# Chunked attention and a soft mixture of experts on one core: the work of a step in another order, and the softmax subtraction written in address order

## The chip, the cores and the metric

The kernel runs on one core of a Trainium2 chip. A core has a matrix engine (TensorE, shown as PE, its weight loads as PEld), a vector engine (VectorE, DVE), a scalar engine (ScalarE, ACT), GpSimd (POOL), and SyncE (SP), whose queue here issues every data transfer. Each engine takes its own instructions strictly in the order in which they are written, and waits on semaphores for what others produce. Matrix products land in PSUM, everything else lies in SBUF. The metric is the device time of one execution in microseconds; less is better.

## What is computed

Attention over 4 batches, 8 heads, 768 positions of 64 values, in chunks of 32 queries. Each chunk sees 8 memory keys, 16 positions to its left, itself, and 8 to its right. The result, as a matrix `x` of 3072 rows and 512 columns, goes through a soft mixture of 8 experts with 4 slots each.

```python
# attention, per chunk
scores = scale * np.matmul(q_c, k_full.transpose(0, 1, 3, 2))
a = np.exp(scores - np.max(scores, axis=-1, keepdims=True))
a = a / (np.sum(a, axis=-1, keepdims=True) + 1e-09)
out[:, :, c_start:c_end] = np.matmul(a, v_full)
...
# experts
logits = x @ phi
d = np.exp(logits - logits.max(0, keepdims=True))
d /= d.sum(0, keepdims=True) + 1e-09
slot_input = d.T @ x
...
h = np.maximum(slot_input[e] @ w1[e], 0.0)
slot_out[e] = h @ w2[e]
...
return (c @ slot_out).astype(np.float32)
```

Here `c` is the softmax of the logits over the slots. All numbers are float32.

## The kernel before

The attention is cut into 12 units of 256 rows (`NU`), numbered 0 to 11, and each step `i` of the main loop (lines 387 to 423) finishes unit `i`. One unit passes through these functions, one TensorE group or one short run of VectorE and ScalarE work each:

- `scores` (line 237, TensorE): 32 matrix products into the one PSUM tile `s`. Every product is float32 and stands as two in the trace, so a unit shows 64.
- `softmax` (line 250, VectorE): `mx`, the maxima of 64 keys each, then two subtractions `p` of 128x512 elements, one for each half of the heads, from PSUM `s` to SBUF `p`. The four blocks of keys of a chunk are stored interleaved, so that a subtraction writes every second word of `p`. Before the change the last loop of the subtraction runs over 32 neighbouring words of PSUM, and writes every fourth word of SBUF; the other block follows in a second sweep.
- `exponent` (line 269, ScalarE): the exponential of `p`, in place.
- `normalizer` (line 272, VectorE): `z`, sums of `p` that read every second word, and their reciprocals.
- `transpose_p` (line 279, TensorE, then ScalarE): `pt_ps` in PSUM, and its copies `pt` in SBUF.
- `values` (line 291, TensorE): 64 products in the trace, into the one PSUM tile `a`; `normalize` (line 308, VectorE): `x`, from `a` and `z`.
- `transpose_x` (line 316, TensorE, then ScalarE): `xt_ps` and its copies `xT`.

Two units make a group `G` of 512 rows. In even steps from 2 on the group's `logits` (line 324, TensorE, `l`) follow with `dispatch_max` (VectorE, `stats` and the copy `lT`) and `dispatch_exp` (ScalarE, `d`); in odd steps `dispatch_t` (line 354, `dt_ps`, `dT`), `dispatch` (`D_ps`) and `dispatch_sum` (`D_sb`, VectorE).

`s` and `a` have one buffer each (two PSUM banks each); the other four banks go round among all smaller PSUM tiles. So `scores` of a unit waits for the subtractions of the unit before, and `values` for the `normalize` before it. The order of the calls in the loop body is the order on every engine, because each call is kept in program order (class `InOrder`).

All transfers go through SyncE's queue, in the order of the calls. A unit loads 512 KB of queries, 560 to 592 KB of keys, 512 KB of values (`vw`, tile `v..0`) and 256 KB of values more (`vx`), which go into the tile `v..1` after GpSimd has copied `v..0` into it (`share_v`). There are three buffers of each (`NB`). With the 64 KB of `phi` these are 22.9 MB in all (MB of a million bytes). Expert weights come in 64 pieces of 512 KB, 32 of `w1` and 32 of `w2`, into slabs: 14 of their own (`NW`), then the buffers of keys, queries, values and `x` as units finish with them, 35 in all. `load_w(upto)` (line 176) issues pieces up to a count: 1.5 a step in the first eight steps, later all for which the table `usable` names a slab. `vx` of a unit stands behind the weights of its step in the queue.

After the loop come the last group, the merge of the groups' maxima, the two layers of the experts (`h`, `so`) and two halves of the output (`o`), each stored by a transfer. There a slab is refilled as soon as its piece has been used.

Of the kernel before, what the change touches and what calls it, by code (L numbers as in the profile page):

```python
# [10 lines left out]
F32 = mybir.dt.float32  # L11
AF = mybir.ActivationFunctionType
# [3 lines left out]
P = 128  # L16
B, H, S, D = 4, 8, 768, 64
NPAIR = H // 2
# [4 lines left out]
NU = B * UPB  # L23
# [20 lines left out]
NEG = -1.0e30  # L44
PIECE = 1024
NB = 3
NW = 14
W0 = 1
WRATE = 1.5
WLAST = 8  # L50
# [19 lines left out]
def tile_attn_softmoe(  # L70
# [68 lines left out]
    def load_v(u):  # L139
        e = v_t[u % NB][0]  # L140
        for h in range(2):
            sp.dma_start(e[h:P:2, h], vw[u, 64 * h:64 * h + 64])
# [12 lines left out]
    for d in range(NB):  # L155
        u = NU - NB + d
        flat = k_t[u % NB].rearrange("p a n -> p (a n)")
        freed += [(u - 2, flat[:, 0:PIECE]), (u - 2, flat[:, PIECE:2 * PIECE])]
        freed += [(u - 2, q_t[u % NB].rearrange("p g n -> p (g n)"))]
        if d:  # L160
            freed += [(u, v_t[u % NB][o][:, a]) for o in range(2) for a in range(2)]
    flat_x = [t.rearrange("p u n -> p (u n)") for t in x_t]
    last = (NG - 1) % 2
    freed += [(NU, flat_x[1 - last][:, 0:PIECE]), (NU, flat_x[1 - last][:, PIECE:2 * PIECE])]
    freed += [(NU + 1, flat_x[last][:, 0:PIECE]), (NU + 1, flat_x[last][:, PIECE:2 * PIECE])]
    usable = {i: NW for i in range(NU + 2)}
    for since, s in sorted(freed, key=lambda f: f[0]):
        slabs.append(s)
        for i in range(since, NU + 2):
            usable[i] = len(slabs)  # L170

    pieces = [("w1", e, kc) for e in range(E) for kc in range(NKC)]
# [64 lines left out]
    def scores(u):  # L237
        s_ps = ps.tile([P, NSUB, NPAIR, 2, 2 * CHUNK], F32, tag="S", name=f"s{u}")
        for s in range(NSUB):
            for g in range(NPAIR):  # L240
                for j in range(4):
                    pe.matmul(
                        s_ps[32 * j:32 * j + 32, s, g],
                        lhsT=q_t[u % NB][:, g, P * s + 32 * j:P * s + 32 * j + 32],
                        rhs=key_columns(u, 4 * s + j, g),
                        start=True, stop=True,
                    )
        return s_ps

    def softmax(u, s_ps):  # L250
        if u % UPB == 0:
            dve.memset(s_ps[0:32, 0, :, :, 0:LEFT], NEG)
        if u % UPB == UPB - 1:
            dve.memset(s_ps[96:128, NSUB - 1, :, :, CHUNK - RIGHT:CHUNK], NEG)
        flat = s_ps.rearrange("p s g h n -> p (s g h) n")
        mx = wk.tile([P, 16, 1], F32, tag="mx", name=f"mx{u}")
        dve.tensor_reduce(out=mx[:, :, 0], in_=flat, axis=AX.X, op=ALU.max)
        p = wk.tile([P, 8, 4 * CHUNK], F32, tag="p", name=f"p{u}")
        for h in range(2):
            dve.tensor_tensor(  # L260
                out=p.rearrange("p m (j s h) -> p h m s j", s=2, h=2)[:, h],
                in0=s_ps.rearrange("p s g h (b j) -> p h (s g) b j", b=2)[:, h],
                in1=mx.rearrange("p (m h) o -> p h m o", h=2)[:, h].rearrange(
                    "p m (o z) -> p m o z", z=1).broadcast_to([P, 8, 2, CHUNK]),
                op=ALU.subtract,
            )
        pexp[u] = p

    def exponent(u):
        act.activation(out=pexp[u], in_=pexp[u], func=AF.Exp, scale=SCALE)  # L270

    def normalizer(u):
        z = wk.tile([P, 16, 1], F32, tag="z", name=f"z{u}", bufs=3)
        dve.tensor_reduce(out=z.rearrange("p (m h) o -> p m (h o)", h=2), in_=pexp[u].rearrange("p m (n h) -> p m h n", h=2), axis=AX.X, op=ALU.add)
        dve.tensor_scalar_add(z, z, 1e-9)
        dve.reciprocal(out=z, in_=z)
        rz[u] = z

    def transpose_p(u):
        pt = []  # L280
        pv = pexp[u]
        for s in range(NSUB):
            t_ps = row(4 * P, f"pt_ps{u}_{s}")
            for g in range(NPAIR):
                pe.transpose(t_ps[:, P * g:P * g + P], pv[:, NPAIR * s + g, :], ident)
            t = wk.tile([P, NPAIR, P], F32, tag=f"pt{s}", name=f"pt{u}_{s}")
            act.copy(out=t.rearrange("p g n -> p (g n)"), in_=t_ps)
            pt.append(t)
        return pt
# [18 lines left out]
    def normalize(u, a_ps):  # L308
        dve.tensor_tensor(
            out=x_of(u).rearrange("p s (m d) -> p (s m) d", d=D),  # L310
            in0=a_ps.rearrange("p s g h d -> p (s g h) d"),
            in1=rz[u].broadcast_to([P, 16, D]),
            op=ALU.mult,
        )

    def transpose_x(u):
        for s in range(NSUB):
            t_ps = row(4 * P, f"xt_ps{u}_{s}")
            for kc in range(NKC):
                pe.transpose(t_ps[:, P * kc:P * kc + P], x_of(u)[:, s, P * kc:P * kc + P], ident)  # L320
            xT[2 * u + s] = wk.tile([P, NKC, P], F32, tag="xT", name=f"xT{u}_{s}", bufs=4)
            act.copy(out=xT[2 * u + s].rearrange("p g n -> p (g n)"), in_=t_ps)

    def logits(G):
        l_ps = row(P, f"l{G}")
        for kc in range(NKC):
            for g in range(4):
                pe.matmul(
                    l_ps[32 * g:32 * g + 32, :],
                    lhsT=phi_sb[:, kc, :],  # L330
                    rhs=xT[4 * G + g][:, kc, :],
                    start=(kc == 0), stop=(kc == NKC - 1),
                )
        return l_ps
# [6 lines left out]
    def dispatch_max(G, l_ps):  # L341
        dve.tensor_reduce(out=nmx[G], in_=l_ps, axis=AX.X, op=ALU.max, negate=True)
        if G:
            dve.tensor_tensor(out=nmx[G], in0=nmx[G], in1=nmx[G - 1], op=ALU.min)
        dve.tensor_copy(out=lT[:, G, :], in_=l_ps)

    def dispatch_exp(G, l_ps):
        d = wk.tile([P, P], F32, tag="d", name=f"d{G}")
        act.activation(out=d, in_=lT[:, G, :], func=AF.Exp, bias=nmx[G], scale=1.0, accum_out=zg[G])
        dexp[G] = d  # L350
        if G:
            act.activation(out=alpha[G], in_=nmx[G - 1], func=AF.Exp, bias=nmx[G], scale=-1.0)
# [7 lines left out]
    def dispatch(G):  # L360
        D_ps = row(DM, f"D_ps{G}")
        for g in range(4):
            pe.matmul(
                D_ps[32 * g:32 * g + 32, :],
                lhsT=dT[G][:, 32 * g:32 * g + 32],
                rhs=x_t[G % 2][:, g, :],
                start=True, stop=True,
            )
        return D_ps
# [5 lines left out]
    def dispatch_sum(G, D_ps):  # L375
        if G == 0:
            dve.tensor_copy(out=D_sb, in_=D_ps)
        else:
            dve.scalar_tensor_tensor(out=D_sb, in0=D_sb, scalar=alpha[G], in1=D_ps, op0=ALU.mult, op1=ALU.add)

    for u in range(2):
        softmax(u, scores(u))
        load_k(u + NB)
        load_q(u + NB)
        exponent(u)
    normalizer(0)
    for i in range(NU):
        G = (i - 2) // 2 if i >= 2 else None
        first = i % 2 == 0
        pt = transpose_p(i)  # L390
        if i >= 1:
            transpose_x(i - 1)
        if G is not None and not first:
            dispatch_t(G)
        if i + 2 < NU:
            softmax(i + 2, scores(i + 2))
            exponent(i + 2)
        a_ps = values(i, pt)
        normalize(i, a_ps)
        if i + 1 < NU:  # L400
            normalizer(i + 1)
        if G is not None and first:
            l_ps = logits(G)
            dispatch_max(G, l_ps)
            dispatch_exp(G, l_ps)
        if G is not None and not first:
            D_ps = dispatch(G)
            dispatch_z(G)
            dispatch_sum(G, D_ps)
        if i + 3 < NU:  # L410
            first_k(i + 3)
        if i + 2 < NU:
            share_v(i + 2)
        if i + 5 < NU:
            load_k(i + 5)
            load_q(i + 5)
        if i + 3 < NU:
            load_v(i + 3)
        load_w(W0 + int(WRATE * (i + 1)) if i < WLAST else usable[i])
        if i + 2 < NU:  # L420
            load_vx(i + 2)
        if i == NU - NB + 1:
            pool.memset(hT, 0.0)
# [1 line left out]
    l_ps = logits(NG - 1)  # L425
    dispatch_max(NG - 1, l_ps)
    dispatch_exp(NG - 1, l_ps)
    load_w(usable[NU])

# [15 lines left out]
    wrow = wk.tile([P, 1], F32, tag="wrow", name="wrow", bufs=1)  # L447
    act.activation(out=wrow, in_=nm, func=AF.Exp, bias=nmt, scale=-1.0)
    dispatch_sum(NG - 1, D_ps)
    load_w(usable[NU + 1])  # L450
    selw = wk.tile([P, NSLOT], F32, tag="selw", name="selw", bufs=1)
    dve.tensor_scalar(out=selw, in0=sel, scalar1=wrow, scalar2=None, op0=ALU.mult)
    si_ps = row(NKC * NSLOT, "si_ps").rearrange("p (c s) -> p c s", c=NKC)
# [184 lines left out]
```

## Time and profile before

| what | value |
|---|---|
| median of 3 runs | 205.89 us (204.71 to 209.38) |
| profiled execution, its own time | 206.37 us |
| its span, first to last instruction | 204.6 us |
| TensorE busy | 153.1 us, 75% |
| VectorE busy | 100.4 us, 49% |
| ScalarE busy | 61.0 us, 30% |
| GpSimd busy | 33.6 us, 16% |
| moved by transfers | 63.11 MB, mean 309 GB/s |

A time in the rows counts from the span's start. In the chain of waits each piece is what the next one waited for; the pieces are merged, and in order of time. In the timeline a row is a run of equal instructions, and the bracket at its end is the idle time just before it with what ended that. A matrix product's end is modelled and reaches into the next product, so that for TensorE the distance between two starts tells more than a duration. All instructions bear line 64, that of the helper which records them, so they are told apart by the names of their tiles.

### The profile page before, as it was taken

Reading aid. Unit: us, or ns where it says so; the run is one execution under the profiler, and the core shown is the slowest. Engines: PE = TensorE matmul, PEld = TensorE weight load, DVE = VectorE, ACT = ScalarE, POOL = GpSimd, SP = SyncE. Lnnn points to the kernel's source line nnn. Section 1 sums busy time; section 2 is a strip of 40 time slices with the busy share of each in tenths; the row PEclk is TensorE's granted clock in tenths of the full one; section 3 lists DMA queues with packets and bytes.
Section 4 is the critical chain, followed back from the end, with each engine's and each line's share of the span. In section 5 each row is a group of like instructions: output and inputs, shape, how many; then the busy total and the mean of one; then the engine's idle time right before and its main releaser. Section 6 shows DMA issues by size and latency. Waiting matters only on the chain.

```text
span 204.6 us, 6085 instructions
## 1 busy us (share of the span) xinstructions
PE 153.1 (75%) x2639; PEld 110.0 (54%) x2639; DVE 100.4 (49%) x168; ACT 61.0 (30%) x115; POOL 33.6 (16%) x42
## 2 busy tenths in 40 slices
PE   5629767887894888579858587688999976699551
PEld 5518656776693757467756374444556642344220
DVE  7063887392879097748926653321460103310331
ACT  7510351425142532335250505300222203210331
POOL 5343134032122402141233000000000000000000
PEclk9999999696999699999988999955999996559955
DMA  6998999998599479925889969996999999998275
GB/s 231 341 350 275 302 390 353 324 308 285 169 325 390 181 211 346 395 105 175 291 242 380 420 192 323 307 385 203 295 407 419 405 405 410 409 412 356 114 301 210
DMA packets 18218, 63.11 MB, mean 309 GB/s; under 512 B 3088, under 2 KB 3088, under 8 KB 18192
## 3 DMA queue, kind: packets, MB, share of 16 engines
q1 hardware_dynamic: 18192, 62.73, 84.2%
q8 instruction: 21, 0.34, 0.7%
q14 instruction: 5, 0.04, 0.1%
HBM read 56.43 MB, written 6.29 MB: 307 GB/s over the span
## 4 chain that ended last, share of the span: by engine, by line
PE 49%; DVE 26%; DMA 15%; ACT 4%; issue 3%; SPq 1%; ACTq 0%; POOLq 0%
PE s L64 12%; PE so L64 8%; PE h L64 8%; DVE p L64 7%; DMA k<-in_k_dram 7%; PE o L64 6%; DVE x L64 5%; DMA v<-in_vx_dram 5%; DVE mx L64 4%; PE a L64 4%; PE xt_ps L64 4%; DMA w<-in_w_dram 4%; DVE z L64 3%; DVE w L64 2%; PE D_ps L64 1%
## 5 line engine op out<-in xcount | busy, mean ns | idle before, releaser
L64 PE MATMUL s<-k,q 128*32 128x128 f32 x768 | 32.6, 340 | 7.4 <-DMA k<-in_k_dram 5.3
L64 PEld LDWEIGHTS s<-k,q 128*32 128x32 f32 x768 | 27.9, 138 | 10.8 <-issue 7.3
L64 POOL COPY v<-v 128x2048 f32<-128x2048 f32 x12 | 22.8, 1898 | 58.5 <-DMA v<-in_vw_dram 26.6
L64 ACT ACTIVATE p<-p 128x1024 f32<-128x1024 f32 x12 | 12.7, 1058 | 63.4 <-DVE p L64 63.4
L64 PE MATMUL a<-v,pt 128*32 128x128 f32 x768 | 24.1, 273 | 3.4 <-DMA v<-in_vx_dram 2.4
L64 PE MATMUL xt_ps<-ident,x 128*128 128x128 f32 x96 | 14.9, 288 | 15.4 <-DVE x L64 7.2
L64 DVE TENSOR_TENSOR p<-s,mx 128x512 f32<-128x512 f32 x24 | 24.6, 1108 | 0.4
L64 PEld LDWEIGHTS a<-v,pt 128*32 128x32 f32 x768 | 21.6, 111 | 4.2 <-issue 3.9
L64 DVE TENSOR_REDUCE mx<-s 128x16 f32<-128x1024 f32 x12 | 14.7, 1225 | 13.4 <-PE s L64 13.1
L64 PEld LDWEIGHTS xt_ps<-ident,x 128*128 128x128 f32 x96 | 10.5, 144 | 19.7 <-DVE x L64 9.7
L64 PE MATMUL o<-shl,v 32*128 32x256 f32 x96 | 12.7, 612 | 8.7 <-DVE w L64 3.9
L64 DVE TENSOR_TENSOR x<-a,z 128x1024 f32<-128x1024 f32 x12 | 14.6, 1217 | 7.3 <-PE a L64 7.3
L64 PE MATMUL pt_ps<-ident,p 128*128 128x128 f32 x96 | 14.1, 292 | 1.0 <-issue 1.0
L64 DVE TENSOR_REDUCE z<-p 128x16 f32<-128x1024 f32 x12 | 14.5, 1208 | 0.0
L64 PEld LDWEIGHTS pt_ps<-ident,p 128*128 128x128 f32 x96 | 11.0, 147 | 6.3 <-PE a L64 2.5
L64 ACT COPY xT<-xt_ps 128x512 f32<-128x512 f32 x24 | 13.0, 601 | 2.8 <-PE xt_ps L64 2.8
L64 PEld LDWEIGHTS o<-shl,v 32*128 32x128 f32 x96 | 5.3, 262 | 15.4 <-DVE w L64 6.5
L64 ACT COPY pt<-pt_ps 128x512 f32<-128x512 f32 x24 | 12.6, 576 | 0.0
L64 DVE MEMSET s<- 32x128 f32 (+1 forms) x8 | 1.1, 138 | 23.3 <-PE s L64 23.3
L64 PE MATMUL l<-xT,phi_sb 128*32 128x128 f32 x192 | 7.5, 274 | 2.4 <-issue 2.3
L64 DVE COPY so_sb<-so 128x256 f32<-128x256 f32 x2 | 0.8, 424 | 15.4 <-PE so L64 15.4
L64 PE MATMUL h<-w,siT 128*32 128x256 f32 x112 | 8.2, 455 | 0.0
(96 smaller groups left out, 157.9 us busy)
## 6 DMA issues: line engine op xcount, KB each, us to landing
w<-in_w_dram SPq DMA_DIRECT2D x28, 512.0 KB, 7.0
v<-in_w_dram SPq DMA_DIRECT2D x14, 512.0 KB, 7.7
q<-in_qT_dram SPq DMA_DIRECT2D x12, 512.0 KB, 6.1
v<-in_vw_dram SPq DMA_DIRECT2D x24, 256.0 KB, 5.5
k<-in_w_dram SPq DMA_DIRECT2D x12, 512.0 KB, 10.2
v<-in_vx_dram SPq DMA_DIRECT2D x24, 128.0 KB, 5.9
q<-in_w_dram SPq DMA_DIRECT2D x6, 512.0 KB, 10.3
out_dram<-w SPq DMA_DIRECT2D x6, 512.0 KB, 2.9
```

Source lines behind the costliest of these rows:

```text
L64: return self.tc.keep_in_program_order(f(*args, **kwargs))
```

## The change

The edits, in four parts:

1. In a step TensorE now runs: transpose of the old `x` (unit `i-1`), `values(i)`, the logits or the dispatch, `scores(i+2)`, and transpose of `p` for unit `i+1`, which was the first group of step `i+1` before. VectorE runs `normalize(i)`, the group's work, `softmax(i+2)` and `normalizer(i+1)`. ScalarE runs `exponent(i+1)` a step later than before.
2. `load_v(i+3)` moves up, to right behind `normalize(i)`, and is followed by a first `load_w`; a second `load_w` stays at the end of the step. The table `usable` counts half steps, and frees the key and query buffers half a step earlier.
3. `dispatch_exp` reads the logits from PSUM, not from the copy `lT`. The copies `pt` have one buffer instead of two, which makes room for a 15th weight slab; there are then 36 slabs.
4. The subtraction's loops are swapped: the two blocks alternate for every key, so that it reads PSUM with jumps of 32 words (128 bytes) and back, and writes every second word of `p` in rising order.

```diff
-NW = 14
+NW = 15
...
-        freed += [(u - 2, flat[:, 0:PIECE]), (u - 2, flat[:, PIECE:2 * PIECE])]
-        freed += [(u - 2, q_t[u % NB].rearrange("p g n -> p (g n)"))]
+        freed += [(2 * u - 3, flat[:, 0:PIECE]), (2 * u - 3, flat[:, PIECE:2 * PIECE])]
+        freed += [(2 * u - 3, q_t[u % NB].rearrange("p g n -> p (g n)"))]
         if d:
-            freed += [(u, v_t[u % NB][o][:, a]) for o in range(2) for a in range(2)]
+            freed += [(2 * u, v_t[u % NB][o][:, a]) for o in range(2) for a in range(2)]
...
-                out=p.rearrange("p m (j s h) -> p h m s j", s=2, h=2)[:, h],
-                in0=s_ps.rearrange("p s g h (b j) -> p h (s g) b j", b=2)[:, h],
+                out=p.rearrange("p m (j s h) -> p h m j s", s=2, h=2)[:, h],
+                in0=s_ps.rearrange("p s g h (b j) -> p h (s g) j b", b=2)[:, h],
...
-            t = wk.tile([P, NPAIR, P], F32, tag=f"pt{s}", name=f"pt{u}_{s}")
+            t = wk.tile([P, NPAIR, P], F32, tag=f"pt{s}", name=f"pt{u}_{s}", bufs=1)
...
-        act.activation(out=d, in_=lT[:, G, :], func=AF.Exp, bias=nmx[G], scale=1.0, accum_out=zg[G])
+        act.activation(out=d, in_=l_ps, func=AF.Exp, bias=nmx[G], scale=1.0, accum_out=zg[G])
...
         softmax(u, scores(u))
         load_k(u + NB)
         load_q(u + NB)
-        exponent(u)
+        if u == 0:
+            exponent(u)
+    pt = transpose_p(0)
     normalizer(0)
     for i in range(NU):
...
-        pt = transpose_p(i)
         if i >= 1:
             transpose_x(i - 1)
+        if i + 1 < NU:
+            exponent(i + 1)
         if G is not None and not first:
             dispatch_t(G)
-        if i + 2 < NU:
-            softmax(i + 2, scores(i + 2))
-            exponent(i + 2)
         a_ps = values(i, pt)
-        normalize(i, a_ps)
-        if i + 1 < NU:
-            normalizer(i + 1)
         if G is not None and first:
             l_ps = logits(G)
+        if G is not None and not first:
+            D_ps = dispatch(G)
+        normalize(i, a_ps)
+        if i + 3 < NU:
+            load_v(i + 3)
+        load_w(W0 + int(WRATE * (i + 0.5)) if i < WLAST else usable[2 * i])
+        if G is not None and first:
             dispatch_max(G, l_ps)
             dispatch_exp(G, l_ps)
         if G is not None and not first:
-            D_ps = dispatch(G)
             dispatch_z(G)
             dispatch_sum(G, D_ps)
+        if i + 2 < NU:
+            softmax(i + 2, scores(i + 2))
+        if i + 1 < NU:
+            pt = transpose_p(i + 1)
+            normalizer(i + 1)
```

TensorE, step 3 (units 2 to 5; the number behind a tile's name is its unit or group, the last number its buffer; `values` of unit 3 goes on in rows that are left out). Before:

```order
L64 MATMUL pt_ps3_0_597<-ident_94,p3_406 128x128 x4
L64 MATMUL pt_ps3_1_604<-ident_94,p3_406 128x128 x4
L64 MATMUL xt_ps2_0_611<-ident_94,x1_77 128x128 x4
L64 MATMUL xt_ps2_1_618<-ident_94,x1_77 128x128 x4
L64 MATMUL dt_ps0_625<-ident_94,d0_584 128x128
L64 MATMUL s5_629<-k2_69,q2_66 32x128 x32
L64 MATMUL a3_669<-v00_70,pt3_0_602 32x128
...
L64 MATMUL D_ps0_707<-x0_76,dT0_627 32x512 x4
```

After, the same step up to the transposes of unit 4's `p`:

```order
L64 MATMUL xt_ps2_0_611<-ident_95,x1_77 128x128 x4
L64 MATMUL xt_ps2_1_618<-ident_95,x1_77 128x128 x4
L64 MATMUL dt_ps0_626<-ident_95,d0_544 128x128
L64 MATMUL a3_630<-v00_70,pt3_0_589 32x128
...
L64 MATMUL D_ps0_663<-x0_76,dT0_628 32x512 x4
L64 MATMUL s5_673<-k2_69,q2_66 32x128 x32
L64 MATMUL pt_ps4_0_712<-ident_95,p4_581 128x128 x4
L64 MATMUL pt_ps4_1_719<-ident_95,p4_581 128x128 x4
```

`scores` of unit 5 went from ahead of `values` of unit 3 to behind it and behind the dispatch, and the transposes of `p` of unit 4 close the step in which those of unit 3 had opened it.

VectorE, the same step. Before:

```order
L64 TENSOR_REDUCE mx5_663<-s5_629 128x16
L64 TENSOR_TENSOR p5_665<-s5_629,mx5_663 128x8x2x32 x2
L64 TENSOR_TENSOR x1_77<-a3_669,z3_561 128x1024
L64 TENSOR_REDUCE z4_703<-p4_523 128x16
L64 TENSOR_SCALAR z4_703<-z4_703 128x16
L64 RECIPROCAL z4_703<-z4_703 128x16
L64 COPY D_sb_93<-D_ps0_707 128x512
```

After:

```order
L64 TENSOR_TENSOR x1_77<-a3_630,z3_598 128x1024
L64 COPY D_sb_94<-D_ps0_663 128x512
L64 MEMSET s5_673 32x8x8
L64 TENSOR_REDUCE mx5_707<-s5_673 128x16
L64 TENSOR_TENSOR p5_709<-s5_673,mx5_707 128x512 x2
L64 TENSOR_REDUCE z4_726<-p4_581 128x16
L64 TENSOR_SCALAR z4_726<-z4_726 128x16
L64 RECIPROCAL z4_726<-z4_726 128x16
```

`x` of unit 3 and the group's sum moved ahead of unit 5's maxima and subtractions; the subtraction's output is now one run of 512.

SyncE's queue, steps 8 and 9: from unit 11's `vw` (tile `v20`) to unit 11's `vx` (tile `v21`). Before:

```order
L64 DMA v20_74<-in_vw_dram 64x1024 x2
L64 DMA w13_91<-in_w1_dram 128x1024
L64 DMA k0_67<-in_w1_dram 128x1024 x2
L64 DMA q0_64<-in_w1_dram 128x1024
L64 DMA k1_68<-in_w1_dram 128x1024 x2
L64 DMA q1_65<-in_w1_dram 128x1024
L64 DMA v11_73<-in_vx_dram 32x1024 x2
L64 DMA k2_69<-in_w1_dram 128x1024 x2
L64 DMA q2_66<-in_w1_dram 128x1024
L64 DMA v21_75<-in_vx_dram 32x1024 x2
```

After:

```order
L64 DMA v20_74<-in_vw_dram 64x1024 x2
L64 DMA w13_91<-in_w1_dram 128x1024
L64 DMA w14_92<-in_w1_dram 128x1024
L64 DMA k0_67<-in_w1_dram 128x1024 x2
L64 DMA q0_64<-in_w1_dram 128x1024
L64 DMA k1_68<-in_w1_dram 128x1024 x2
L64 DMA q1_65<-in_w1_dram 128x1024
L64 DMA v11_73<-in_vx_dram 32x1024 x2
L64 DMA k2_69<-in_w1_dram 128x1024 x2
L64 DMA q2_66<-in_w1_dram 128x1024
L64 DMA v21_75<-in_vx_dram 32x1024 x2
```

Seven pieces of weights stood ahead of unit 10's `vx` (tile `v11`), now eight; the first five of these, and the `vw`, are issued in the middle of step 8, where all stood at its end before.

## Rows read from the trace of the kernel before

**Rows 1.** Page of the profile, part 2: 40 slices of 5.1 us each.

```profile
PEclk9999999696999699999988999955999996559955
...
GB/s 231 341 350 275 302 390 353 324 308 285 169 325 390 181 211 346 395 105 175 291 242 380 420 192 323 307 385 203 295 407 419 405 405 410 409 412 356 114 301 210
```

**Rows 2.** Chain of waits, units 4 and 5: start us, us, what.

```profile
57.62 1.93 PE s L64 x64
...
59.62 0.18 DVE s L64
...
61.08 2.16 DVE p L64 x2
63.24 1.05 DVE x L64
...
66.25 0.21 DVE lT L64
...
67.69 0.33 PE dt_ps L64
68.02 3.57 PE s L64 x64
...
77.26 1.93 PE s L64 x64
```

**Rows 3.** Timeline, TensorE: start us, us, engine, line, operation, out<-in, shapes, count.

```profile
73.10 1.03 PE L64 MATMUL D_ps<-x,dT 128*32 128x512 f32 x8
...
93.29 1.09 PE L64 MATMUL pt_ps<-ident,p 128*128 128x128 f32 x8
...
94.22 1.16 PE L64 MATMUL xt_ps<-ident,x 128*128 128x128 f32 x8
...
95.31 1.95 PE L64 MATMUL s<-k,q 128*32 128x128 f32 x64
...
97.08 1.93 PE L64 MATMUL a<-v,pt 128*32 128x128 f32 x64
...
98.83 1.06 PE L64 MATMUL l<-xT,phi_sb 128*32 128x128 f32 x32
```

**Rows 4.** Groups of VectorE by form: busy us, mean ns | idle before, releaser.

```profile
L64 DVE TENSOR_TENSOR p<-s,mx 128x512 f32<-128x512 f32 x24 | 24.6, 1108 | 0.4
L64 DVE TENSOR_REDUCE mx<-s 128x16 f32<-128x1024 f32 x12 | 14.7, 1225 | 13.4 <-PE s L64 13.1
...
L64 DVE TENSOR_REDUCE z<-p 128x16 f32<-128x1024 f32 x12 | 14.5, 1208 | 0.0
...
L64 DVE TENSOR_REDUCE stats<-l 128x1 f32<-128x128 f32 x6 | 1.4, 239 | 2.2 <-PE l L64 2.2
...
L64 DVE TENSOR_TENSOR v<-c_ps,cm 128x384 f32<-128x384 f32 x2 | 1.1, 558 | 0.1
...
L64 DVE TENSOR_REDUCE nms<-nm_ps 32x32 f32<-32x128 f32 x1 | 0.3, 279 | 1.0 <-PE nm_ps L64 1.0
```

**Rows 5.** Timeline around units 9 to 11 and the experts, SyncE's queue and TensorE.

```profile
99.06 1.12 SPq L64 DMA_DIRECT2D v<-in_vw_dram  x2
...
106.44 1.46 SPq L64 DMA_DIRECT2D v<-in_vx_dram  x2
...
117.65 1.84 PE L64 MATMUL a<-v,pt 128*32 128x128 f32 x59 [2.41 <-DMA v<-in_vx_dram]
...
124.55 1.96 PE L64 MATMUL a<-v,pt 128*32 128x128 f32 x64
...
139.46 5.39 PE L64 MATMUL h<-w,siT 128*32 128x256 f32 x64
...
179.38 1.08 PE L64 MATMUL so<-w,v 128*32 128x256 f32 x8
```

**Rows 6.** Timeline of the start, TensorE.

```profile
18.35 1.95 PE L64 MATMUL pt_ps<-ident,p 128*128 128x128 f32 x8
...
23.65 1.96 PE L64 MATMUL a<-v,pt 128*32 128x128 f32 x64
```

More of the change, by code (lines that the diff above doesn't have):

```diff
@@ L157, in tile_attn_softmoe @@
         flat = k_t[u % NB].rearrange("p a n -> p (a n)")
-        freed += [(u - 2, flat[:, 0:PIECE]), (u - 2, flat[:, PIECE:2 * PIECE])]
-        freed += [(u - 2, q_t[u % NB].rearrange("p g n -> p (g n)"))]
+        freed += [(2 * u - 3, flat[:, 0:PIECE]), (2 * u - 3, flat[:, PIECE:2 * PIECE])]
+        freed += [(2 * u - 3, q_t[u % NB].rearrange("p g n -> p (g n)"))]
         if d:
-            freed += [(u, v_t[u % NB][o][:, a]) for o in range(2) for a in range(2)]
+            freed += [(2 * u, v_t[u % NB][o][:, a]) for o in range(2) for a in range(2)]
     flat_x = [t.rearrange("p u n -> p (u n)") for t in x_t]
     last = (NG - 1) % 2
-    freed += [(NU, flat_x[1 - last][:, 0:PIECE]), (NU, flat_x[1 - last][:, PIECE:2 * PIECE])]
-    freed += [(NU + 1, flat_x[last][:, 0:PIECE]), (NU + 1, flat_x[last][:, PIECE:2 * PIECE])]
-    usable = {i: NW for i in range(NU + 2)}
+    freed += [(2 * NU, flat_x[1 - last][:, 0:PIECE]), (2 * NU, flat_x[1 - last][:, PIECE:2 * PIECE])]
+    freed += [(2 * NU + 1, flat_x[last][:, 0:PIECE]), (2 * NU + 1, flat_x[last][:, PIECE:2 * PIECE])]
+    usable = {i: NW for i in range(2 * NU + 2)}
     for since, s in sorted(freed, key=lambda f: f[0]):
         slabs.append(s)
-        for i in range(since, NU + 2):
+        for i in range(since, 2 * NU + 2):
             usable[i] = len(slabs)
@@ L260, in softmax @@
             dve.tensor_tensor(
-                out=p.rearrange("p m (j s h) -> p h m s j", s=2, h=2)[:, h],
-                in0=s_ps.rearrange("p s g h (b j) -> p h (s g) b j", b=2)[:, h],
+                out=p.rearrange("p m (j s h) -> p h m j s", s=2, h=2)[:, h],
+                in0=s_ps.rearrange("p s g h (b j) -> p h (s g) j b", b=2)[:, h],
                 in1=mx.rearrange("p (m h) o -> p h m o", h=2)[:, h].rearrange(
-                    "p m (o z) -> p m o z", z=1).broadcast_to([P, 8, 2, CHUNK]),
+                    "p m (o z) -> p m o z", z=1).broadcast_to([P, 8, CHUNK, 2]),
                 op=ALU.subtract,
@@ L416, in tile_attn_softmoe @@
             load_q(i + 5)
-        if i + 3 < NU:
-            load_v(i + 3)
-        load_w(W0 + int(WRATE * (i + 1)) if i < WLAST else usable[i])
+        load_w(W0 + int(WRATE * (i + 1)) if i < WLAST else usable[2 * i + 1])
         if i + 2 < NU:
@@ L427, in tile_attn_softmoe @@
     dispatch_exp(NG - 1, l_ps)
-    load_w(usable[NU])
+    load_w(usable[2 * NU])
     nm = nmx[NG - 1]
@@ L449, in tile_attn_softmoe @@
     dispatch_sum(NG - 1, D_ps)
-    load_w(usable[NU + 1])
+    load_w(usable[2 * NU + 1])
     selw = wk.tile([P, NSLOT], F32, tag="selw", name="selw", bufs=1)
```

## Prediction

> **What bounds the kernel now.** I read the page first. TensorE is busy for three quarters of the span, but the granted clock falls again and again in the attention, and the transfers swing between 105 and 420 GB/s [rows 1]. Neither engine nor queue is full there; something makes them take turns. So I went to the chain of waits. It goes round a ring: scores of unit 6 on TensorE at 57.62, then 6.84 us of VectorE without a gap (59.62 to 66.46: maxima, two subtractions, `x`, `z`, the group's logits), then TensorE's transposes, and scores again at 68.02 and 77.26 [rows 2]. Two steps take 77.26 - 57.62 = 19.64 us. VectorE works while TensorE waits for `x` of the unit before, whose transposes stand ahead of the next scores, and then TensorE works while VectorE waits for these scores. [...]
>
> What would a step cost without the ring? By starts in the timeline of TensorE, transposes of `p` take 94.22 - 93.29 = 0.93 us, of `x` 1.09, scores 1.77, values 1.75; by durations 1.09, 1.16, 1.95 and 1.93. Logits add 1.06, the dispatch 1.03 and its transpose 0.33 [rows 2, 3]. Two steps are 2 x 5.54 + 2.42 = 13.50 by starts and 2 x 6.13 + 2.42 = 14.68 by durations, 6.75 to 7.34 a step. VectorE needs 6.84. Both are far below 19.64 / 2 = 9.82.
>
> **The change, part by part.** I follow the end of `values` from unit to unit, and then the tail.
>
> *Start.* Before, scores of unit 2 stood ahead of values of unit 0, which ran from 23.65 to 25.61; the transposes of `p` ended at 20.30 [rows 6]. Now values come next. Their end lies between 20.30 + 1.96 = 22.3 and 25.6 (if the extra values are late); I take 22.3, since at 23.65 they had not been waited for.
>
> *The order of a step.* Behind values of unit i TensorE now has 1.06 (logits) or 1.03, then scores and the transposes of the next `p`, about 4 us in all, before it needs `x` of unit i. VectorE makes that `x` in 1.05 us [rows 2] at once, since the maxima of unit i+2 now stand behind it. So the wait for `x` goes. What is late next is one of two: VectorE's 6.84 us, to which some waiting for scores comes when it is ahead (under 1.06 + 1.77 - 1.05 = 1.8), or TensorE's 6.75 to 7.34. I take 7.2 a step: TensorE hides VectorE's work, or the reverse, and it hardly matters which. If that cover went, a step would be back at the ring's 9.8. The first two steps have no group: 7.2 - 2.42 / 2 = 6.0. Values of unit 2 then end at 22.3 + 2 x 6.0 = 34.3, of unit 3 at 41.5.
>
> *The subtraction.* 24 of 1108 ns [rows 4]; by the chain two take 2.16 us. The trace shows neither access by itself on this shape. Reading every second word of SBUF is free: `z` does it in 1208 ns, `mx` reads neighbours in 1225, both 1024 elements. Reading PSUM with a jump of 128 bytes at every element is in one small row, `nms` over 32 partitions: 279 ns for 128 elements, against 239 for 128 neighbours in `stats`. That is 0.3 ns an element, 0.16 us for 512. A full-rate subtraction from PSUM took 558 ns for 384 elements, some 700 for 512 [rows 4]. So one costs from 0.70 (if every second word is written freely) to 1.11 + 0.16 = 1.27 us (if the writes stay as they are and the jump is added); I take 0.85, nearest to the rows of `z` and `nms`. This brings VectorE to 6.84 - 0.5 = 6.3 a step, and none of it counts, for TensorE needs 6.75. At 1.27 VectorE would need 7.2, which is what I took.
>
> [...]
>
> *Logits from PSUM, one `pt` buffer, a 15th slab.* ScalarE no longer waits for `lT` (0.21 us), off the path. The copies `pt` of unit i+1 wait for values of unit i, which end 4 us earlier, so nothing. The slab saves one of 29 late pieces; nothing by itself.
>
> *The queue.* It becomes the next limit. Unit 3's `vx` comes behind units 0 to 3 whole, queries and keys of units 4 to 6, `vw` of unit 4 and four weight pieces: 13.6 MB. The first eight slices of 5.115 us moved 13.1 MB, the ninth gets past 13.6 at 42.5 us [rows 1]. The last `vx` comes behind everything else the attention loads, 22.9 MB, and 24 pieces of weights, 12.6 MB: 35.5 MB, 21.9 more. At TensorE's pace values of unit 10 would start about 41.5 + 7 x 7.2 - 1.9 = 90.0. Before, unit 10's `vx` decided: issued at 106.44 behind seven pieces, values went on at 117.65, 18.6 us after values of unit 8 had ended at 99.01 [rows 3, 5]. In the new order values of unit 8 end at 41.5 + 5 x 7.2 = 77.5, eight pieces and 0.8 MB (5.0 MB) follow. At the 380 to 420 GB/s of the slices from 107 to 117 us that is 12 to 13 us, and with some 3 us for issue and landing values of unit 10 start at 93, end at 95, and values of unit 11, after logits, transposes and dispatch transpose (1.06 + 1.09 + 1.16 + 0.33), at 100.6. By bytes: 21.9 MB from 42.5 us on at 350 to 400 GB/s (slices that had work to do show 341 to 420) take 55 to 63 us, so the last `vx` is there at 98 to 106 and values of unit 11 end at 100 to 108. I take 375 GB/s: 42.5 + 58.4 + 1 to land + 1.9 = 103.8. The queue is later than the engines by 3 us, and it sets the end of the attention. GpSimd's copies of `v` stand ahead of each `vx`, as before.
>
> *The tail* has the same instructions: from the end of values of unit 11, 124.55 + 1.96 = 126.51, to the first expert product at 139.46 is 12.95 us, from there to the end of the span 204.6 - 139.46 = 65.1 [rows 5]. Twelve slabs (6.3 MB, 16 us at 400) come after the last `vx` and are used last of the first layer, so they are in time.
>
> Sum: 103.8 + 12.95 + 65.1 = 181.9 us of span. The profiled execution took 206.37 with a span of 204.6; with the same 1.8 us around it 183.7, against a median of 205.89 before, to which the profiled run lies within 0.3%. I round to 183.5.
>
> **Rivals.**
>
> *The engines alone set it (faster still).* If the queue runs at 410 GB/s and starts better, values of unit 11 end near 97 to 100: 177 to 180 us. For it: the 405 to 419 of the slices from 148 us on [rows 1]; against it: these move nothing but whole 512 KB pieces with nobody to wait for.
>
> *The queue keeps its mean.* If dependences (a copy on GpSimd ahead of every `vx`, few transfers in flight) hold it at the mean of the page, 309 GB/s, the 21.9 MB take 71 us, values of unit 11 end at 116.4 and the execution at 196. For it: the swings in the attention, down to 105. Against it: the low slices are those where TensorE waited in the ring, which held back the release of buffers.
>
> *VectorE becomes the limit, and the kernel slower.* The place is the subtraction's jumping read of PSUM. A step needs 6.84 - 2.16 + 2s us with s for one subtraction; it passes 7.2 at s = 1.26. At 2.0 a step is 8.7 and the execution some 11 x 1.5 = 16 us longer than the engines' 180, 196 us. Slower than before it gets only when the gain of some 22 us is eaten: 2s = 7.2 + 22 / 11 - 4.68, s = 2.3, twice what it takes now; 2.5 for slower by over 2%. Against it: 0.3 ns an element in `nms`. [...]
>
> *No change that counts.* The attention ends earlier but the experts wait for weights: 28 pieces, 14.7 MB, follow once slabs come free, 36 us at 405 GB/s, against 40 us from the first expert product to the first use of the last 16 pieces, at 179.38 [rows 5]. It fits, by 3 us; a loss here is small.
>
> **How the numbers follow.** The forecast, with its own range from 179 to 189, has a chance of 0.55, the engines alone 0.15, the queue at its mean (or a subtraction of 1.5 to 2.0 us) 0.22, no change 0.04, slower 0.04. So faster by over 2%, about what a measurement of this kernel can tell from no change, 0.92; same 0.04; slower 0.04. The range goes from 176 to 197.
>
> **What would show it.** In the new trace: no wait of TensorE for `x` or `lT`; scores of all units but the first two near 1.95 us and a granted clock near 1.0 up to unit 9; two steps in 14 to 15 us; a subtraction between 0.70 and 1.27; values of units 10 and 11 waiting for `vx`; values of unit 11 ending near 104; the first expert product 13 us later and 65 us to the end. I am wrong in the cause if TensorE waits elsewhere in every step, in the size if `vx` of units 2 and 3 or 10 and 11 are late by much, and altogether if subtractions take over 2 us.

## The result, and the profile after

The changed kernel takes 193.67 us (median of 4 runs, 191.69 to 194.17) against 205.87 before: a ratio of 0.941, 95% interval 0.931 to 0.950. The profiled execution took 193.99 us with a span of 192.2. It is faster, within the range given, but 10.3 us above the sum for the profiled execution (183.7). In all ratios below, disturbed runs are left out on both sides, so that a ratio can differ by a per cent from that of two medians.

The page of the changed kernel, parts 2 and 3 (slices of 4.8 us; the last line is the queue that the page names `instruction`: packets, MB, share of 16 engines):

```profile
PEclk9999999999999997899999699756999996579755
...
GB/s 227 362 355 244 315 381 384 414 357 339 236 292 331 385 320 297 302 345 263 300 396 416 182 309 313 372 368 304 374 413 413 407 408 408 414 414 117 208 234 218
...
q8 instruction: 21, 0.34, 0.7%
```

The clock now stays at nine tenths or more up to 72 us, where [rows 1] fell every few slices, and then falls behind two idle times of TensorE (2.81 us from 71.29, 4.94 us from 101.3, below): it is 0.83 on the mean from 70 to 80 us, and again from 100 to 110. Behind the 3.18 us that end at 35.51 it stays, at 1.00 from 30 to 40 us. The transfers swing as before, from 182 to 416 GB/s.

The chain of waits of the changed kernel (start us, us, what), against [rows 2]:

```profile
40.34 1.94 issue
...
48.21 1.48 issue
...
54.40 6.46 DMA v<-in_vx_dram
...
71.29 2.81 issue
74.10 1.20 PE s L64 x25
...
96.73 9.35 DMA v<-in_vx_dram
106.08 0.14 issue
106.22 3.07 PE a L64 x59
...
112.88 1.95 PE a L64 x64
114.84 0.02 issue
114.86 1.24 DVE x L64
...
126.74 6.53 PE h L64 x64
```

The ring is gone: between 40 and 114 us the chain lists no piece of VectorE work. Two other things take its place. One is `vx`, the extra values, that come late (54.40 and 96.73). The other is TensorE standing still in the middle of a group of equal products, waiting for nothing the profile shows ("issue", 1.5 to 2.8 us each).

VectorE's groups by form (busy us, mean ns | idle before), against [rows 4]:

```profile
L64 DVE TENSOR_TENSOR p<-s,mx 128x512 f32<-128x512 f32 x24 | 15.6, 692 | 0.4
...
L64 DVE COPY x<-o 128x512 f32<-128x512 f32 x4 | 2.8, 692 | 5.4 <-PE o L64 5.4
```

A subtraction takes 692 ns where it took 1108, to the nanosecond what the plain copies of 512 words out of PSUM (`x<-o`) take.

TensorE's timeline of the changed kernel (the bracket: idle just before, and what ended it), against [rows 3, 5]:

```profile
19.70 2.09 PE L64 MATMUL a<-v,pt 128*32 128x128 f32 x64
...
35.51 1.84 PE L64 MATMUL a<-v,pt 128*32 128x128 f32 x59 [3.18 <-DMA v<-in_vx_dram]
37.14 0.31 PE L64 MATMUL a<-v,pt 128*32 128x128 f32 x3
...
74.10 1.20 PE L64 MATMUL s<-k,q 128*32 128x128 f32 x25 [2.81 <-issue]
...
84.99 1.95 PE L64 MATMUL a<-v,pt 128*32 128x128 f32 x64
...
106.22 3.07 PE L64 MATMUL a<-v,pt 128*32 128x128 f32 x59 [4.94 <-DMA v<-in_vx_dram]
...
112.81 1.96 PE L64 MATMUL a<-v,pt 128*32 128x128 f32 x64
```

Values of unit 0 end at 21.8 (19.70 + 2.09), of unit 2 at 37.45, of unit 8 at 87.0 (the row at 84.99), of unit 11 at 114.8. The first expert product follows 11.9 us later, the end of the span 65.5 us after that.

SyncE's queue in steps 6 and 8 (start us, us, transfer):

```profile
69.38 1.47 SPq L64 DMA_DIRECT2D v<-in_vw_dram  x2
75.34 1.87 SPq L64 DMA_DIRECT2D k<-in_k_dram  x2
...
78.41 1.11 SPq L64 DMA_DIRECT2D v<-in_vx_dram  x2
...
94.30 0.45 SPq L64 DMA_DIRECT2D q<-in_w_dram  x1
95.47 1.74 SPq L64 DMA_DIRECT2D v<-in_vx_dram  x2
```

Between 70.85 and 75.34 the queue issues nothing: its next entry is the keys of unit 11, whose buffer is read by the scores that TensorE was stuck in until 75.3. All that stands behind waits as well. The last row is `vx` of unit 10, 8.5 us after values of unit 8 ended, behind eight pieces of weights.

### The profile page after: what moved, and what is told of

It reads as the page before. It is cut to its first block, busy times and chain, and to the rows that moved or that the text cites. A ratio compares the mean times of both kernels' runs of the same rounds, so it can differ in the third digit from the quotient of the medians.

```text
span 192.2 us, 6090 instructions
## 1 busy us (share of the span) xinstructions
PE 147.8 (77%) x2639; PEld 108.3 (56%) x2639; DVE 97.9 (51%) x168; ACT 61.9 (32%) x115; POOL 33.7 (18%) x42
## 4 chain that ended last, share of the span: by engine, by line
PE 46%; DMA 32%; DVE 7%; issue 5%; SPq 5%; ACT 2%; POOL 1%; ACTq 0%; POOLq 0%; DVEq 0%
DMA v<-in_vx_dram 12%; PE h L64 9%; PE a L64 9%; PE o L64 6%; DMA k<-in_k_dram 6%; PE s L64 5%; DMA k<-in_w_dram 5%; SPq L64 5%; PE so L64 4%; DMA w<-in_w_dram 4%; DMA q<-in_qT_dram 4%; PE pt_ps L64 3%; PE xt_ps L64 2%; PE D_ps L64 2%; DVE x L64 2%
## 5 line engine op out<-in xcount | busy, mean ns | idle before, releaser
L64 PE MATMUL s<-k,q 128*32 128x128 f32 x768 | 28.3, 299 | 11.1 <-issue 5.8
L64 PE MATMUL a<-v,pt 128*32 128x128 f32 x768 | 26.5, 284 | 10.3 <-DMA v<-in_vx_dram 9.6
L64 PEld LDWEIGHTS s<-k,q 128*32 128x32 f32 x768 | 24.8, 120 | 14.9 <-issue 11.6
L64 DVE TENSOR_TENSOR x<-a,z 128x1024 f32<-128x1024 f32 x12 | 14.7, 1225 | 16.0 <-PE a L64 15.5
L64 PE MATMUL pt_ps<-ident,p 128*128 128x128 f32 x96 | 15.0, 304 | 1.9 <-issue 1.9
L64 DVE TENSOR_TENSOR p<-s,mx 128x512 f32<-128x512 f32 x24 | 15.6, 692 | 0.4
L64 PEld LDWEIGHTS o<-shl,v 32*128 32x128 f32 x96 | 5.4, 265 | 15.5 <-DVE v L64 5.4
L64 PE MATMUL xt_ps<-ident,x 128*128 128x128 f32 x96 | 13.5, 282 | 0.7 <-DVE x L64 0.5
L64 ACT ACTIVATE d<-l,stats 128x128 f32<-128x128 f32 x6 | 2.2, 368 | 25.1 <-DVE lT L64 12.1
L64 PE MATMUL h<-w,siT 128*32 128x256 f32 x120 | 9.8, 499 | 0.0
L64 POOL COPY k<-k 128x192 f32<-128x192 f32 (+2 forms) x20 | 5.8, 294 | 18.9 <-DMA k<-in_k_dram 18.9
L64 ACT ACTIVATE hs<-h,rzd 128x512 f32<-128x512 f32 x4 | 2.7, 687 | 17.6 <-PE h L64 17.6
```

The source lines that it names most:

```text
L64: return self.tc.keep_in_program_order(f(*args, **kwargs))
```

## The experiments

Three theories. Theory 1: the rate of the transfers sets the attention. Theory 2: the engines do. Theory 3: the place of `vx` in the queue does. The experiments are numbered in the order in which they ran.

**Which of the two edits did it (experiments 2 and 3).** Experiment 2 is the changed kernel with the old loops, experiment 3 the old kernel with the new ones (the edit of experiment 2; that of experiment 3 is its reverse).

```diff
-out=p.rearrange("p m (j s h) -> p h m j s", s=2, h=2)[:, h],
-in0=s_ps.rearrange("p s g h (b j) -> p h (s g) j b", b=2)[:, h],
+out=p.rearrange("p m (j s h) -> p h m s j", s=2, h=2)[:, h],
+in0=s_ps.rearrange("p s g h (b j) -> p h (s g) b j", b=2)[:, h],
...
```

> The changed kernel with the subtraction's loops as before (two subtractions about 2.2 us a unit instead of 1.4). Theory 1 (the queue sets the steps) and theory 3 (the place in the queue): the same within 1%, 192 to 196. Theory 2 with VectorE as the engine that sets the step: 11 x 0.83 = 9 us more, near 203.

> The kernel before with only the subtraction's loops swapped. If the ring of VectorE and TensorE set the steps before, as the prediction says: 0.83 us less in each of about 10 steps, 197 to 199 against 205.9. If the queue set them before as well: within 1% of before.

Experiment 2: 194.20 us, ratio to before 0.944 (0.936 to 0.952). In VectorE's groups its subtraction is slow again:

```profile
L64 DVE TENSOR_TENSOR p<-s,mx 128x512 f32<-128x512 f32 x24 | 25.7, 1165 | 0.4
```

Ten more microseconds of VectorE cost the kernel half a microsecond, which lies within the intervals. They are not without trace: VectorE stands in this run's chain again (`mx` and `p` of four units between 41.67 and 80 us), and values of unit 8 end at 88.5 instead of 87.0. What is left is covered by the wait for `vx` of unit 10, behind which values go on at 106.98 here and at 106.22 in the changed kernel. Experiment 3: a median of 198.03 us, ratio 0.958 (0.945 to 0.970), which is 197.0 by before's 205.7, where 197 to 199 was expected of the ring; the interval goes from 194 to 200. So either the order alone (0.944) or the subtraction alone (0.958) shortens the kernel, and both together give 0.941. That fits two edits that work on the same ring; a part of it may be that `vx` of unit 10 comes late in all three. VectorE doesn't set the new step, and theory 2 in its VectorE form falls. Whether the subtraction would count once `vx` comes early was not tried.

**Fewer bytes (experiment 1).** It shows which part bytes have.

```diff
 def load_q(u):
-    sp.dma_start(q_t[u % NB], qT[u])
+    if u < NB:
+        sp.dma_start(q_t[u % NB], qT[u])
```

> The queries of units 3 to 11 are not loaded (the scores use those of units 0 to 2 again), so 9 x 512 KB = 4.7 MB less goes through the queue; every engine's work and the order of everything else stay. Theory 1 (the transfer queue, at some 330 GB/s, sets the steps): 4.7 MB / 330 GB/s = 14 us less, values of unit 11 end near 101 instead of 114.8, median 179 to 182. Theory 2 (the engines set the steps, the stalls inside TensorE's groups among them): within 2 us of the changed kernel's 193.7. Theory 3 (the place of the extra values behind other loads in the queue, not the bytes): the waits for the extra values of units 2, 5 and 10 shrink only by what the queries took there, at most 5 us in all, 189 to 192.

Ratio 0.892 (0.881 to 0.903), some 183.5 us by before's 205.7; values of unit 11 end at 103.18 + 1.95 = 105.1. The gain of 10 us lies between theories 1 and 3; neither stands alone. The queue moved fewer bytes, and not faster: 299 GB/s from 42.5 to 106 us, against 326 in the changed kernel.

**Another order of the same bytes (experiments 4, 7 and 9).** Experiment 4 takes `vx` ahead of everything else at the step's end:

```diff
-        if i + 3 < NU:
-            first_k(i + 3)
         if i + 2 < NU:
             share_v(i + 2)
+            load_vx(i + 2)
+        if i + 3 < NU:
+            first_k(i + 3)
         if i + 5 < NU:
             load_k(i + 5)
             load_q(i + 5)
         load_w(W0 + int(WRATE * (i + 1)) if i < WLAST else usable[2 * i + 1])
-        if i + 2 < NU:
-            load_vx(i + 2)
```

> The changed kernel with the copy and the load of the extra values of unit i+2 ahead of the keys and queries of unit i+5 and of the step's second load of weights. The same bytes in another order. Theory 1 (the rate of the queue alone): the same within 1%. Theory 3 (the extra values stand behind loads that wait for the scores of unit i+2 and behind weights that nobody needs yet): the waits of values for the extra values of units 2, 5 and 10 (3.2 + 1.5 + 4.9 us) go, and the kernel gains 5 to 9 us, 185 to 189. Theory 2 (engines): within 2 us.

185.17 us, ratio 0.898 (0.889 to 0.908), 4.5% below the changed kernel. The same stretch in both, first the changed kernel, then experiment 4 (busy times, granted clock, share of the transfer engines, GB/s):

```profile
42.50:106.00 63.50, 51.13 (x1157) 43.71 (x1155) 48.35 (x74) 27.17 (x53) 17.33 (x17) 0.97 0.92 326
```

```profile
42.50:106.00 63.50, 52.96 (x1218) 45.30 (x1219) 46.37 (x78) 26.92 (x55) 17.37 (x18) 1.00 1.00 373
```

So the same loads can go at 373 GB/s. What holds them at 326 is read in what SyncE's queue waited for (us in total, times, longest), again the changed kernel and then experiment 4:

```profile
SPq L64 <- PE a L64: 15.3, 9, 4.0
...
SPq L64 <- PE s L64: 9.9, 6, 4.3
```

```profile
SPq L64 <- PE a L64: 5.2, 3, 3.6
...
SPq L64 <- PE s L64: 0.7, 2, 0.4
```

25 us of standing still for TensorE became 6; waits for GpSimd's copies grew from 3.6 us to 7.0. Theory 1, as a rate that the loads can't pass, falls. Experiment 7 divides this gain: `vx` moves ahead of the weights only, and stays behind keys and queries.

```diff
-        load_w(W0 + int(WRATE * (i + 1)) if i < WLAST else usable[2 * i + 1])
         if i + 2 < NU:
             load_vx(i + 2)
+        load_w(W0 + int(WRATE * (i + 1)) if i < WLAST else usable[2 * i + 1])
```

> The changed kernel with the extra values of unit i+2 ahead of the step's second load of weights, but still behind the keys and queries of unit i+5. It divides the gain of experiment 4 (8.5 us). If weights ahead of the extra values cost it: values of units 10 and 11 come early and 185 to 187. If the queue's standing still for the scores of unit i+2, whose buffers the keys need, cost it: 191 to 194. Half and half: 188 to 190, with values of unit 5 still waiting 1.5 us and values of unit 10 under 1.

186.71 us, 0.916 (0.905 to 0.927). TensorE's timeline of experiment 7:

```profile
34.20 3.42 PE L64 MATMUL a<-v,pt 128*32 128x128 f32 x59 [3.25 <-DMA v<-in_vx_dram]
...
97.14 0.38 PE L64 MATMUL s<-k,q 128*32 128x128 f32 x2 [3.60 <-issue]
99.35 1.99 PE L64 MATMUL a<-v,pt 128*32 128x128 f32 x61
```

The wait of unit 10 (4.94 us) is gone, that of unit 2 stays (3.25), behind keys and queries. Most of the gain, 7 of 8.5 us, is the weights that stood ahead of `vx`, which nobody needs for another 20 us (values of unit 10 went on at 106.22 in the changed kernel, the first expert product came at 126.7); the rest is within the intervals. The queue still stood still for TensorE for 17.9 us (9.1 and 8.8), and moved 341 GB/s in the same stretch. So what stands behind the waiting entries counts for more than how long the queue stands. Experiment 9 goes on that way: experiment 4 without the load of weights in the middle of a step.

```diff
-        load_w(W0 + int(WRATE * (i + 0.5)) if i < WLAST else usable[2 * i])
```

> Experiment 4 without the load of weights in the middle of a step: each step loads all its pieces at its end, behind the extra values, keys and queries. The bytes are the same. If the weights ahead of the extra values still cost something (waits of 3.7 us, 0.55 of them for values of unit 10): 183 to 184.5. If the full transfer engines set the step (373 GB/s from 42.5 to 106 us at a share of 1.0): the same as experiment 4, 184 to 186, for they move the same in another order.

186.86 us, 0.924 (0.904 to 0.944): above both expectations, and no gain over experiment 4.

**Earlier still (experiment 8).** The copy and load of `vx` go to the middle of the step.

```diff
         normalize(i, a_ps)
+        if i + 2 < NU:
+            share_v(i + 2)
+            load_vx(i + 2)
         if i + 3 < NU:
             load_v(i + 3)
```

> The changed kernel with the copy and load of the extra values of unit i+2 in the middle of step i, ahead of the values of unit i+3 and of all weights of the step, half a step earlier than in experiment 4. If the extra values are still late there (3.7 us of waits): 182 to 184. If the remaining step is TensorE's: 184 to 186 as in experiment 4. If the queue now waits for GpSimd's copy, and the values of unit i+3 come late for it: 188 or more.

195.95 us, 0.961 (0.946 to 0.975), worse than the changed kernel. In its timeline TensorE waits for GpSimd in five steps (one row stands here), and at the end for the last `vx`:

```profile
68.94 1.29 PE L64 MATMUL s<-k,q 128*32 128x128 f32 x38 [0.83 <-POOL k L64]
...
114.12 3.42 PE L64 MATMUL a<-v,pt 128*32 128x128 f32 x59 [7.38 <-DMA v<-in_vx_dram]
```

and SyncE's queue stands behind GpSimd's copies:

```profile
SPq L64 <- POOL k L64: 28.6, 10, 4.3
```

The view names `k`, but in the step of the scores at 68.94 GpSimd's copy of `v`, which had waited 7.58 us for `vw`, ended at 68.42 us, and the queue's next transfer, `vx`, was issued at 68.44. The copies of `first_k`, which these scores need, came behind it on GpSimd. The entry moved up in the queue took its own waits with it: 28.6 us for GpSimd, where the same line of the changed kernel shows 3.6.

**The weights out of the way (experiment 5).** Both `load_w` calls of the loop are dropped; the pieces follow after it.

> The changed kernel with all pieces of weights but the first loaded only after the loop, so that the attention's own 22.9 MB have the queue to themselves; the median says nothing (the experts then wait), only when values of unit 11 end (114.8 us in the changed kernel). If bytes or the weights ahead of the extra values held the attention: 100 us or earlier. If the engines hold it: 112 to 115. TensorE's idle time inside a group of equal products (8.4 us in five pieces, the largest 2.8): if it is the fetch of its instructions held up behind data in full transfer engines, the pieces shrink below 0.5 us each; if it is anything of the engine's own, they stay at 1 to 3 us.

TensorE's timeline of experiment 5:

```profile
33.87 2.99 PE L64 MATMUL a<-v,pt 128*32 128x128 f32 x59 [2.75 <-DMA v<-in_vx_dram]
36.57 0.49 PE L64 MATMUL a<-v,pt 128*32 128x128 f32 x3
...
69.45 0.95 PE L64 MATMUL s<-k,q 128*32 128x128 f32 x25 [1.79 <-issue]
...
99.88 1.95 PE L64 MATMUL a<-v,pt 128*32 128x128 f32 x64
```

The one run took 196.61 us, 81 of them in the experts, most of whose weights are asked for only then. Values of unit 11 end at 101.8, 13 us earlier, and from unit 2 (37.1) to unit 11 a step takes 64.7 / 9 = 7.2 us. The idle pieces inside groups sum to 2.15 us (0.36 and 1.79) against 8.4. On the pieces neither expectation came true: three of five went, and one stayed at 1.79.

**What the idle pieces are.** The trace has a record of each packet of the queue q8. In the changed kernel the idle pieces end shortly after one of them (us; a table of my own from these records):

```
idle from  to     packet from  to     end of idle after packet
27.10  27.73      25.37  26.30        1.43
40.34  42.27      39.75  40.75        1.52
48.21  49.69      47.43  48.39        1.30
71.29  74.10      71.81  72.70        1.40
97.10  98.64      96.40  97.37        1.27
```

The old kernel, the changed one and experiments 1, 2 and 4 to 11 have 49 idle pieces from 15 us on with nothing shown, and every one ended 1.20 to 1.62 us after a packet had landed. A packet has 16,384 bytes (21 of them make the 0.34 MB of the page). If the 21 packets carry TensorE's 2639 products and as many weight loads, each has some 126 products (2639 / 21, an estimate: no record shows what a packet holds). The pieces lie at the same places of the program, while their times differ: counted from the first product, within two, behind 345, 471, 597, 723, 1102, 1229, 1355, 1481, 1606, 1734 or 1861, that is in steps of 126. So it is in the old order too, where other products stand at these places (product 1230 is one of `logits` there, and of `scores` in the changed kernel), and the packets fit in number too: the piece behind 345 ends after the second packet, the one behind 1229 after the ninth, and so with all 49. My reading is that TensorE has run out of instructions there, and goes on when the next packet is in; what was measured is the places and the 1.20 to 1.62 us. Experiments 3 and 12 add ten pieces, of which nine fit; the tenth, and one ahead of 15 us in experiment 11, lie in the start (ending at 18.89 and 12.48 us), at none of these places.

**Does that go away with fewer bytes? (experiments 6, 10 and 11).** Experiment 6 is experiment 4 with the edit of experiment 1. Experiments 10 and 11 are experiment 9 with a steady rate of weights:

```diff
-        load_w(W0 + int(WRATE * (i + 1)) if i < WLAST else usable[2 * i + 1])
+        load_w(min(usable[2 * i + 1], W0 + int(WRATE * (i + 1))))
```

and in experiment 11 `WRATE = 1.0` besides.

> Experiment 4 (extra values ahead of keys and queries) without the loads of queries of units 3 to 11. If bytes still set the step there: 4.7 MB at the 380 GB/s that its queue now reaches, 12 us less than its 185.2, near 173 to 175. If TensorE's own work and its stalls set it: at most 4 us less, 181 to 185.

> Experiment 9 with 1.5 pieces of weights a step to the end of the loop, 19 in all instead of up to 36, the rest after the loop: some 7 MB less go through the queue before the extra values of unit 11 are needed. If the full transfer engines set the step: values of unit 11 end at 99 to 101 (104.2 in experiment 4), 180 to 182. If TensorE with its stalls sets it whatever the queue carries: 184 to 186. If the experts then wait for weights: longer than 65 us from the first expert product to the end, by what they wait.

> As experiment 10 with 1 piece a step, 13 at the end of the loop. TensorE's idle time inside groups shrinks further if it is the fetch of instructions behind data (6.2 us in experiment 4, 2.2 us in experiment 5 with no weights): values of unit 11 end at 97 to 100. The remaining 51 pieces, 26.7 MB, take 65 us at 410 GB/s, until 165 to 168, and the last 16 are used from about 155 on: the experts wait some us in the second layer. So 178 to 182 if they wait little, 183 to 187 if the weights become the end.

Experiment 6: 179.67 us, 0.881 (0.866 to 0.896), between the two expectations; idle pieces 6.4 us, with 4.7 MB less than experiment 4, which has 6.2. Experiment 10: 183.16, 0.901 (0.885 to 0.918), between its first two expectations, with values of unit 11 at 104.0 and idle pieces of 1.3 us in the profiled execution. Experiment 11: 184.59, 0.902 (0.868 to 0.936); in its profiled execution (185.04 us, the fastest took 181.54) the idle pieces sum to 6.8 us with the least weights of the three. So fewer bytes alone don't make the idle pieces shrink, as experiment 6 shows: the expectation of experiment 11 missed. Each sum is that of one execution. What decides when the next packet comes stays open.

**A version to keep (experiment 12).** Experiment 10 with the first `vx` of the loop taken into the part before it:

```diff
         if u == 0:
             exponent(u)
+            share_v(2)
+            load_vx(2)
...
-        if i + 2 < NU:
+        if 0 < i < NU - 2:
             share_v(i + 2)
             load_vx(i + 2)
```

> Experiment 10 with the copy and load of the extra values of unit 2 ahead of the keys and queries of unit 4, in the part before the loop. The same bytes. Values of unit 2 waited 1.83 us for them in experiment 10. If that wait still counts at the end: 181 to 182.5 against its 183.2, ratio to before near 0.89. If later waits take it up (values of units 6 and 9, 0.38 and 1.90 us): the same as experiment 10 within 1%. If the keys of unit 4 come late behind the copy: 184 or more.

183.22 us, ratio 0.897 (0.889 to 0.905). The wait went, and values of unit 11 ended at 100.8 instead of 104.0. But the experts then took 69.4 us instead of 64.7. Their timeline (second layer) and a stretch of it:

```profile
140.35 0.64 PE L64 MATMUL so<-w,v 128*32 128x256 f32 x8 [0.55 <-DMA w<-in_w_dram]
141.70 0.64 PE L64 MATMUL so<-w,v 128*32 128x256 f32 x8 [0.71 <-DMA w<-in_w_dram]
```

```profile
138.00:160.00 22.00, 14.89 (x134) 5.85 (x126) 4.58 (x7) 3.88 (x7) 0.00 (x0) 0.65 1.03 409
```

Now the experts wait for weights, four times and 2.1 us in all, with the transfer engines full (a share of 1.03, 409 GB/s); experiment 10 has no such wait. The other 2.6 us of the 4.7 are not settled; in the first 4.8 us of the experts the granted clock was 0.54, against 0.70 in experiment 10. Experiments 4, 10 and 12 end at 183 to 185 us; they beat both kernels, and no difference among them is shown.

## Why the prediction was right in kind and 10 us off

- *The ring.* Right. The wait for `x` left the chain, and the order alone gives 0.944. Experiment 3, at 197.0 by its ratio, came out where the ring's size put it.
- *The subtraction.* Right that it counts for nothing in the new order (0.944 against 0.941), as long as `vx` of unit 10 is what comes late. The value taken, 0.85 us, was too high: 0.692 is the lower bound of 0.70. Against a plain copy (692 ns) neither the jumping read of PSUM nor writing every second word shows a cost (692 ns as well). That the slow form pays for writing every fourth word is argued, and not shown: it also writes in rows of 32 where the fast form has one run of 512, and no run tells the two apart.
- *7.2 us a step.* Right for the engines: 7.2 in experiment 5 (7.0 without its idle piece of 1.79 us). In the changed kernel six steps from unit 2 to unit 8 took 87.0 - 37.45 = 49.6 us, 8.3 each. Of these, 6.2 us (1.94 + 1.48 + 2.81) are idle pieces inside groups and 1.5 is `vx` of unit 5; without them a step is 7.0. The idle pieces were no term of the sum. They were to be seen: TensorE's timeline of the old kernel has three pieces of "issue", 4.4 us in all, which the prediction passed over:

```profile
83.45 0.86 PE L64 MATMUL l<-xT,phi_sb 128*32 128x128 f32 x24 [2.34 <-issue]
...
91.00 1.39 PE L64 MATMUL a<-v,pt 128*32 128x128 f32 x42 [0.98 <-issue]
...
112.64 1.10 PE L64 MATMUL pt_ps<-ident,p 128*128 128x128 f32 x8 [1.05 <-issue]
```

- *The start.* Values of unit 0 ended at 21.8 against 22.3. Values of unit 2 ended 3.1 us late, for `vx` of unit 2 was 3.2 us late behind the keys and queries of units 3 to 5; the prediction reckoned with the engines alone until unit 3.
- *The queue.* The step that failed: "I take 375 GB/s: 42.5 + 58.4 + 1 to land + 1.9 = 103.8". Values of unit 11 ended at 114.8. The 1 us to land was an estimate that no run shows by itself: from its issue to its landing a transfer of `vx` took 5.9 us in the old kernel and 6.3 in the changed one (medians of 24). That the queue is next, that unit 10 waits for `vx` and that the pieces ahead of it decide it was right (experiment 7); unit 11 did not wait. The rate was not wrong as a property of the transfers (experiment 4 reached 373) but as a property of this order: with entries that wait for TensorE at its head the queue moved 326 GB/s. Put into the sum, 326 gives 112.6, 8.8 of the 11 us that were missing. How much of it is the idle pieces, which hold the scores that the queue waits for (70.85 to 75.34), no run separates. From the end of values of unit 8 until unit 10's went on behind `vx` it took 19.2 us, where the count of the pieces had given 15.5. The rival "the queue keeps its mean" (values of unit 11 at 116.4) came nearer. Its reason, dependences, was right in kind, but those that it names were not the ones: the queue stood 25.2 us for TensorE and 4.8 for GpSimd's copies (3.6 and 1.2). The argument against it, that the slow slices came only from the ring, was wrong.
- *The tail.* 11.9 us against 12.95, then 65.5 against 65.1. Right.

In sum over the forecast: 3.1 us up to unit 2, 6.4 from there to unit 8, 1.5 to unit 11, -1.05 and +0.4 behind, 10.3 us by unrounded numbers. These are not independent: experiment 7 took 7 us off with the idle pieces still in (9.6 us in its profile), because it took away the wait of unit 10.

## What to carry to other kernels

The queue of this kernel, which issues in order, had two limits: its bytes (4.7 MB less gave some 10 us in experiment 1), and the waits at its head (326 GB/s with 25.2 us of standing still for TensorE, 373 with 5.9). Before giving such a queue a rate, list for each late load what stands ahead of it, what those entries wait for, and who needs them; loads that nobody needs yet belong behind those that the next step waits for, but an entry moved up brings its own waits (28.6 us for GpSimd in experiment 8). And look in the old trace for idle time inside a group of equal instructions: here it was 4.4 us beside the waits of the ring, and 8.4 us when these were gone.

## What was not expected of the hardware

TensorE stood still inside groups of equal products for up to 3.94 us at a time (experiment 11), and all 49 such pieces from 15 us on, in the two kernels and experiments 1, 2 and 4 to 11, ended 1.20 to 1.62 us after a packet of 16,384 bytes of the queue q8 had landed; in the changed kernel's attention they were 8.4 us. The places lie in steps of 126 products, in the old order and in the new. That TensorE waits there for the instructions in the packet is a reading of these numbers, and not shown by a record. VectorE's subtraction of 512 words ran at 692 ns reading PSUM with jumps of 128 bytes and writing every second word of SBUF, against 1108 (old kernel) and 1165 ns (experiment 2) reading neighbours and writing every fourth, in rows of 32.
